# Turning q on VectorE too, in place, with half the blocks moved from a GpSimd copy

## The chip, the cores and the metric

The kernel runs on one core of one Trainium2 chip. A core has TensorE (matmuls, records PE, with weight loads PEld), VectorE (DVE), ScalarE (ACT), GpSimd (POOL) and SyncE (SP), which here only issues DMAs. All run their own instructions in order and wait for each other through semaphores. The metric is the device time of the whole kernel in microseconds (us); lower is better. Times of "before" are three runs; the profile is one more execution.

## The reference

Two parts, in float32. First attention over 8 batches and 8 heads, 576 tokens and 64 values per head, in which scores that lie more than `tau` below the row's maximum are dropped:

```python
scores = scale * np.matmul(q, k.transpose(0, 1, 3, 2))
thresh = np.max(scores, axis=-1, keepdims=True) - tau
scores = np.where(scores >= thresh, scores, -1000000000.0)
scores = scores - np.max(scores, axis=-1, keepdims=True)
attn = np.exp(scores)
attn = attn / (np.sum(attn, axis=-1, keepdims=True) + 1e-09)
return np.matmul(attn, v).astype(np.float32)
```

Its output, reordered to 4608 tokens of 512 values, goes through a feed-forward layer (512 to 1024 to 512) with a SoLU activation and a layer norm between:

```python
h = x @ w_in
e = np.exp(h - np.max(h, axis=-1, keepdims=True))
sm = e / (np.sum(e, axis=-1, keepdims=True) + 1e-09)
solu = h * sm
mu = np.mean(solu, axis=-1, keepdims=True)
var = np.mean((solu - mu) ** 2, axis=-1, keepdims=True)
ln = (solu - mu) / np.sqrt(var + 1e-06) * g_ln
return (ln @ w_out).astype(np.float32)
```

## The kernel before

**Tiling.** Two heads make a pair: head 0 on partitions 0 to 63, head 1 on 64 to 127. There are 32 pairs, numbered `i = 4 * batch + hp`. For scores, q and k must lie with the 64 values of a head along the partitions (`qT`, `kT`), while they come from memory with tokens along the partitions, so both must be turned. Of the 576 query tokens of a head, 512 are done in four slots of 128 (`kind` 0 and 1, `r` 0 and 1); the last 64, the tails (`qe`), of four pairs are gathered in two more slots (`kind` 2). This gives 18 slots per batch (`PER`) and 144 in all (`NS`).

**Rounds.** A hand-written loop at the end of the kernel issues everything for one slot per round, `rnd`; `tc.manual_schedule()` keeps the order. In round `rnd`:

- TensorE makes the scores of slot `rnd` (L451, two heads into two score banks `s_ps`). VectorE takes the maxima (`maxes`, L473), ScalarE the ramp that keeps or drops (L488), which is the last reader of a score bank, and the exponential (L497).
- GpSimd normalises the slot before (`normalise`, L504 to L507). VectorE turns it in 32x32 blocks (`blocks`, L519), and on every second slot four DMAs put it as `wT` (L530) where the product with v reads it, three rounds later (L555). ScalarE copies the product out to `xh` or `xe` (L578).
- TensorE also does a quarter of a feed-forward tile of 128 tokens: two rounds of first-layer halves (`ff_h`, L611), then two rounds of the output product (`ff_o`, L715). In between come, spread over later rounds, maximum and exponential (L626, L635), product (L641), statistics (`ff_stats`: L656 on VectorE, then five small GpSimd instructions), normalisation (`ff_norm` L677 on ScalarE, `ff_norm2` L682 on VectorE), a swap of blocks by four DMAs (`ff_swap`, L693, `V<-u`), and a VectorE transpose (`ff_turn`, L703, `uT`). Between two first-layer halves a small memset on GpSimd (`fence`, L108, `mark`) is waited for by TensorE.

**How q and k are turned.** For batches 0 and 1 TensorE multiplies 64x64 blocks by the identity (`turn`, L318), and ScalarE and VectorE copy the results from PSUM to `qT`, `kT`, `qe` (L351, L355, L376, L395, L399); q is scaled by `scl` on the way. In later rounds these products go to a spare part of the score banks, ahead of the scores of the same round; `preps` holds the items with their rounds.

From batch 2 on k goes another way. `load_natural` (L186) loads a pair of k in four DMAs of 32 partitions, three rounds ahead. `turn_natural` has VectorE transpose it in 32x32 blocks to a buffer `flip` (L191), and two DMAs bring it to `kT` (L194). Its place is the end of the round in `turn_at`: after `blocks` and the `late` jobs. q of these batches is still turned by TensorE: `load_one` loads half a batch (L130) and the tails (L141); `q_item` and `e_item` make 16 and 2 products per pair.

**Order of DMAs.** SyncE issues nearly all of them, in program order: in a round first the swap, then `wT`, the stores (L742), the flips, then loads by `load_at`. v comes in four parts per half batch (L158).

**Buffers.** `qT` has 6 buffers of 512 columns, `kT` 7, `qe` 7; `loads` has 2 for q and 2 for k.

Of the kernel before, what the change touches and what calls it, by code (L numbers as in the profile page):

```python
# [16 lines left out]
P = 128  # L17
# [3 lines left out]
def kernel(  # L21
# [127 lines left out]
    def load_v(b, hf, parts=(0, 1, 2)):  # L149
        d = halves.setdefault((b, hf), {})  # L150
        hs = slice(4 * hf, 4 * hf + 4)

        if b > 1:
            if 0 in parts:
                d["v"] = loads.tile([P, 4, NK, D], F32, tag="v", bufs=3, name="v")
            for part in parts:
                two, u = divmod(part, 2)
                nc.sync.dma_start(  # L158
                    out=d["v"][ROWS[u], 2 * two : 2 * two + 2].rearrange("p h m d -> p h (m d)"),
                    in_=v[b, hs][2 * two : 2 * two + 2].rearrange("h (p m) d -> p h (m d)", m=NK),  # L160
                )
            return
        if 0 in parts:
            d["v"] = loads.tile([P, 4, NK, D], F32, tag="v", bufs=3, name="v")
        rest = v[b, hs, 0:SM, :].rearrange("h (p t) d -> p h (t d)", t=4)
        for part, to, rows, of in (
            (0, 0, slice(0, P), slice(0, P)), (1, 4, ROWS[0], ROWS[1]), (1, 4, ROWS[1], ROWS[0])
        ):
            if part in parts:
                nc.sync.dma_start(  # L170
                    out=d["v"][rows, :, to : to + 4].rearrange("p h t d -> p h (t d)"),
                    in_=rest[of],
                )
        for rows in ROWS if 2 in parts else ():
            nc.sync.dma_start(
                out=d["v"][rows, :, NK - 1], in_=v[b, hs, SM:S, :].rearrange("h p d -> p h d")
            )

    def load_natural(i):
        b, hp = divmod(i, NP)  # L180
        src = k[b, 2 * hp : 2 * hp + 2].rearrange("h (i a t) d -> a h i (t d)", a=2, t=NK)
        raw = loads.tile([P, 4, 4, D], F32, tag="k", name="k")
        natural[i] = raw = raw.rearrange("p h t d -> p (h t d)")[:, 0 : NK * D]
        for g in range(4):
            a, h = divmod(g, 2)
            nc.sync.dma_start(out=raw[32 * g : 32 * g + 32], in_=src[a, h])  # L186

    def turn_natural(i):
        raw = natural.pop(i)
        flip = loads.tile([P, 2, NK, 32], F32, tag="flip", bufs=1, name="flip")  # L190
        nc.vector.transpose(out=flip, in_=raw.rearrange("p (t x g) -> p g t x", g=2, x=32))  # L191
        to = pair(i)["kT"]
        for a in range(2):
            nc.sync.dma_start(  # L194
                out=to[:, 32 * NK * a : 32 * NK * (a + 1)],
                in_=flip[ROWS[a]].rearrange("p g t x -> p g (t x)"),
            )

# [113 lines left out]
    def turn(spare, x, lhsT_of, rows=2):  # L312
# [3 lines left out]
        for r in range(rows):  # L316
# [14 lines left out]
    def pair(i):  # L331
        if i not in pairs:
            pairs[i] = dict(
                qT=heads.tile([P, SM], F32, tag="qT", bufs=6, name="qT"),
# [48 lines left out]
    def e_item(i):  # L383
        src, h0 = source(i)
        last = k_parts(i)[:, NK - 1] if i < 2 * NP else None

        def make(spare, x):
            turn(
                spare, x, lambda r, y: ends[i // NP][ROWS[r], 2 * (i % NP) + y],
                2 if i < 2 * NP else 1,  # L390
            )

        def keep(spare, x, r):
# [4 lines left out]
            elif last is not None:  # L398
# [31 lines left out]
    def scores(s, items):  # L430
# [10 lines left out]
        for ks in (slice(SM, S), slice(0, SM)):  # L441
            for h in range(2):
                for y in range(2):
                    if kind < 2:
                        d = pairs[b * NP + hp]
                        t = P * (2 * kind + r) + 64 * y
# [87 lines left out]
    def attend_steps(key):  # L534
# [7 lines left out]
        for e in range(2) if kind == 2 else [None]:  # L542
            for m in range(NK):
                for u in range(2):
                    d, h0 = source(b * NP + (hp if e is None else e + 2 * u))
                    for h in range(2):
                        if e is None:
                            to = y[ROWS[h], u, 0:P].rearrange("p (r g x) -> p g r x", r=2, g=2)
# [13 lines left out]
    def attended(key):  # L562
        b, kind, hp = key
        tag, y = units.pop(key)["y"]
        y = y.rearrange("p (u n) -> p u n", u=2)[:, :, 0:P].rearrange("p u (r y) -> p u r y", r=2)
# [6 lines left out]
        else:  # L572
# [4 lines left out]
            to = xh[b, kind][:, hp].rearrange("p (r u y) -> p u r y", r=2, u=2)  # L577
# [155 lines left out]
    def ff_store(t, last):  # L733
        d = ffn.pop(t)
        if len(t) == 1:
            rows = out.rearrange("(b s) m -> s b m", s=S)[SM:S, 2 * t[0] : 2 * t[0] + 2]
# [25 lines left out]
    for i in range(NP, NPAIR):  # L762
        b, hp = divmod(i, NP)
        if b == 1:
            at = (13, 15, 19, 20)[hp]
        else:
            at = PER * (b - 1) + ((6, 12, 16, 21) if b == 2 else (6, 9, 12, 17))[hp]
        if b == 1:
            preps += [
                (at, 3, lambda i=i: k_item(i, slice(0, 3)), i),  # L770
                (at, 1, lambda i=i: k_item(i, slice(3, 4)), i),
            ]
        preps += [
            (at, 1, lambda i=i: e_item(i), i),
# [4 lines left out]
    turn_at = {}  # L779
# [11 lines left out]
    for i in range(2 * NP, NPAIR):  # L791
        b, hp = divmod(i, NP)
        if b == 2:
            at = (24, 30, 34, 39)[hp]
        else:
            at = PER * b + 4 * hp - (11 if b % 2 else 13)
        turn_at[at] = i
        load_at.setdefault(at - 3, []).append(lambda i=i: load_natural(i))
        if hp % 2:
            load_at.setdefault(PER * (b - 1) + (9 if hp == 3 else -1), []).append(  # L800
                lambda b=b, hf=hp // 2: load_one(b, hf, "q")
            )
# [6 lines left out]
    with tc.manual_schedule():  # L809
# [29 lines left out]
        while True:  # L839
# [61 lines left out]
            if rnd - 1 in pieces:  # L901
                weight_c(pieces[rnd - 1])
            for job in middle.pop(rnd, []):
# [64 lines left out]
            if rnd in turn_at:  # L968
                turn_natural(turn_at[rnd])
            if rnd == 3:  # L970
# [47 lines left out]
```

## Time and profile before

| what | us |
|---|---|
| three runs | 885.73, 885.70, 883.92 |
| median | 885.7 |
| the profiled execution, whole | 883.54 |
| its span, first to last instruction | 881.8 |

The rows of the groups that the change touches, apart from those shown in the prediction:

```profile
L351 ACT ACTIVATE qT<-s_ps,scl 128x256 f32<-128x256 f32 x30 | 14.4, 481 | 0.0
L355 DVE TENSOR_SCALAR qT<-s_ps,scl 128x256 f32<-128x256 f32 x26 | 12.5, 480 | 0.0
L395 ACT ACTIVATE qe<-s_ps,scl 128x64 f32<-128x64 f32 x28 | 8.8, 313 | 0.0
L318 PE MATMUL s_ps<-ident,ends 64*64 64x64 f32 x128 | 8.5, 220 | 0.3 <-DVE both L473 0.3
```

A row names line, engine, operation, output and inputs, shapes and count; then the group's busy time in us and the mean of one in ns; then the idle time of the engine ahead of it and what ended it. Products in float32 appear twice, so 896 records of q are 28 pairs of 16 products. In a timeline a line gives start, length, engine, line and count; a bracket holds the idle time before it.

### The profile page before, as it was taken

The page shows a single profiled execution, that of the slowest core. Times are in us where ns is not written, and L with a number is a line of the kernel's source. Part 1 is how long each engine was busy: PE and PEld are TensorE (multiplying, and loading weights), DVE is VectorE, ACT ScalarE, POOL GpSimd, SP SyncE. Part 2 cuts the span into 40 slices and gives each one's busy share as a digit, 9 for nine tenths or more (in the row PEclk, how much of TensorE's full clock was granted, in tenths as well). Part 3 has the DMA queues.
Part 4 walks back from the last instruction along what each step waited for, and adds up shares of the span by engine and source line. Part 5 has one row for each costly group of instructions (what it writes and reads, how often), then busy time and mean ns, then how long its engine had stood idle before and what let it go on. Part 6 is the DMA issues. An engine that isn't in the chain of part 4 may idle for free. (4 is left out here: it accounts for less than half of the span.)

```text
span 881.8 us, 38016 instructions
## 1 busy us (share of the span) xinstructions
PE 835.4 (95%) x16225; PEld 592.1 (67%) x16225; DVE 682.0 (77%) x1248; ACT 586.3 (66%) x1201; POOL 471.0 (53%) x888
## 2 busy tenths in 40 slices
PE   5667999989999999999999999999999999999997
PEld 3445666665676877677777777777677677777655
DVE  5989788878787888888778887888687888777451
ACT  5977777767666766767677677777676777775121
POOL 2878655545555555555554655555555555555120
PEclk9878899999999999999999999999999999999999
DMA  7999978887878796988789787888779777866222
GB/s 230 254 260 256 218 186 196 217 191 175 201 170 212 178 208 157 206 207 189 158 194 214 184 204 166 208 213 185 165 173 219 182 174 155 186 133 143 65 49 49
DMA packets 85033, 161.60 MB, mean 183 GB/s; under 512 B 19832, under 2 KB 49536, under 8 KB 84864
## 3 DMA queue, kind: packets, MB, share of 16 engines
q1 hardware_dynamic: 83728, 157.18, 76.6%
q8 instruction: 127, 2.08, 1.1%
q10 hardware_dynamic: 1136, 2.00, 0.7%
q14 instruction: 42, 0.34, 0.1%
HBM read 46.14 MB, written 9.44 MB: 63 GB/s over the span
## 5 line engine op out<-in xcount | busy, mean ns | idle before, releaser
L473 DVE CUSTOM_DVE_ANT_0 w<-s_ps,tau_t 128x576 f32<-128x576 f32 x280 | 200.7, 754 | 108.0 <-PE s_ps L451 90.7
L715 PE MATMUL o_ps<-w,uT 64*64 64x256 f32 x4608 | 265.2, 376 | 1.1 <-DVE uT L703 1.1
L488 ACT ACTIVATE w<-s_ps,nth 128x576 f32<-128x576 f32 x280 | 199.8, 743 | 97.0 <-DVE nth L473 93.1
L715 PEld LDWEIGHTS o_ps<-w,uT 64*64 64x64 f32 x4608 | 218.9, 133 | 58.3 <-issue 13.8
L507 POOL TENSOR_SCALAR w<-w,sm 128x576 f32<-128x576 f32 x288 | 218.8, 772 | 14.3
L497 ACT ACTIVATE w<-w,ntau 128x576 f32<-128x576 f32 x288 | 220.3, 772 | 0.0
L611 PE MATMUL h_ps<-w,xh 64*64 64x512 f32 x1856 | 220.0, 596 | 0.0
L519 DVE STREAM_TRANSPOSE T<-w 128x576 f32<-128x576 f32 x288 | 206.3, 752 | 7.4 <-POOL w L507 6.0
L555 PEld LDWEIGHTS pv<-wT,v 64*64 64x64 f32 x5760 | 166.5, 136 | 51.1 <-issue 36.3
L451 PE MATMUL s_ps<-kT,qT 64*64 64x64 f32 (+1 forms) x2048 | 168.1, 422 | 16.4 <-ACT w L488 12.5
L555 PE MATMUL pv<-wT,v 64*64 64x128 f32 (+1 forms) x5760 | 170.9, 263 | 7.9 <-DMA wT<-T 3.7
L611 PEld LDWEIGHTS h_ps<-w,xh 64*64 64x64 f32 x1856 | 98.3, 135 | 96.6 <-issue 88.6
L504 POOL TENSOR_SCALAR sm<-sm 128x2 f32<-128x2 f32 x144 | 36.0, 250 | 229.5 <-ACT w L497 226.4
L505 POOL TENSOR_TENSOR sm<-sm,mone 128x2 f32<-128x2 f32 x144 | 104.6, 726 | 12.0
L677 ACT ACTIVATE V<-u,nb,rs 128x1024 f32<-128x1024 f32 x36 | 44.7, 1241 | 52.2 <-POOL nb L667 52.2
L451 PEld LDWEIGHTS s_ps<-kT,qT 64*64 64x64 f32 x2048 | 61.8, 139 | 25.1 <-ACT w L488 17.7
L578 ACT COPY xh<-pv 128x256 f32<-128x256 f32 x64 | 23.7, 370 | 67.3 <-PE pv L555 67.3
L703 DVE STREAM_TRANSPOSE uT<-V 128x1024 f32<-128x1024 f32 x36 | 44.5, 1236 | 23.7 <-DMA V<-u 23.5
L497 ACT ACTIVATION_READ_ACCUMULATOR w<-w,ntau 128x1 f32 x288 | 56.9, 198 | 0.0
L635 ACT ACTIVATE u<-h_ps,hm 128x1024 f32<-128x1024 f32 x36 | 40.2, 1118 | 21.2 <-DVE hm L626 15.3
L626 DVE TENSOR_REDUCE hm<-h_ps 128x1 f32<-128x1024 f32 x36 | 43.1, 1197 | 12.2 <-PE h_ps L611 6.2
L682 DVE TENSOR_SCALAR u<-u,rs,nb 128x1024 f32<-128x1024 f32 x36 | 42.4, 1178 | 12.7 <-ACT V L677 12.4
(82 smaller groups left out, 590.4 us busy)
## 6 DMA issues: line engine op xcount, KB each, us to landing
wT<-T SPq DMA_DIRECT2D x288, 288.0 KB, 5.9
v<-in_v_dram SPq DMA_DIRECT2D x48, 288.0 KB, 4.8
V<-u SPq DMA_DIRECT2D x144, 64.0 KB, 4.1
out_dram<-ob SPq DMA_DIRECT2D x71, 128.0 KB, 3.1
q<-in_q_dram SPq DMA_DIRECT2D x15, 512.0 KB, 5.9
k<-in_k_dram SPq DMA_DIRECT2D x96, 72.0 KB, 4.6
kT<-flip SPq DMA_DIRECT2D x48, 144.0 KB, 2.7
raw<-in_moe_w_out_dram SPq DMA_DIRECT2D x8, 512.0 KB, 8.2
```

The costliest lines, as they stand in the source:

```text
L451: nc.tensor.matmul(out=ps[h][ROWS[y], ks], lhsT=lhsT, rhs=d["kT"][ROWS[h], ks], start=True, stop=True,)
L473: nc.vector.tensor_tensor_reduce(out=w, in0=ps[:, 0:S], in1=(zero if loose else tau_t).to_broadcast([P, S]), scale=1.0, scalar=BIG, op0=AL ...
L488: nc.scalar.activation(out=d["w"][x], in_=d["w"][x] if d["loose"] else d["ps"][x][:, 0:S], func=AF.Prelu, bias=d["nth"][x], scale=-1.0, al ...
L497: nc.scalar.activation(out=w, in_=w, func=AF.Exp, bias=ntau, scale=1.0, accum_out=sm[:, x : x + 1])
L505: nc.gpsimd.tensor_tensor(out=sm, in0=sm, in1=mone, op=ALU.pow)
L507: nc.gpsimd.tensor_scalar(out=w, in0=w, scalar1=sm[:, x : x + 1], scalar2=1.0, op0=ALU.mult, op1=ALU.mult)
L519: nc.vector.transpose(out=T[:, :, r, h, :], in_=w)
L555: nc.tensor.matmul(out=to, lhsT=d["v"][ROWS[u], h0 + h, m ^ 4 * u if m < 8 and b < 2 else m], rhs=rhs, start=m == 0, stop=m == NK - 1,)
L611: mm = nc.tensor.matmul(out=h[ROWS[y], f], lhsT=x[ROWS[r], c, ROWS[y]], rhs=w1_parts[ROWS[r], c, part ^ r], start=part == 0 and c == 0, st ...
L677: nc.scalar.activation(out=V, in_=u, func=AF.Identity, bias=nb, scale=rs)
L703: nc.vector.transpose(out=uT, in_=d["V"].rearrange("p y (m x) -> p m y x", x=32))
L715: nc.tensor.matmul(out=d["o"][ROWS[z], 512 * r : 512 * r + 256], lhsT=d["uT"][ROWS[r], m].rearrange("p y x -> p (y x)"), rhs=w2[ROWS[r], m ...
```

## The change

From batch 2 on, q takes the way of k, and both take a shorter one:

- **Load.** One DMA for q and one for k per pair, 128 partitions of 9 tokens each (2304 bytes). q is loaded in the round of the previous turn, k a round later.
- **Scale.** GpSimd multiplies q by `scl` in the round of the turn, after `normalise`.
- **Turn.** VectorE transposes k and q in 32x32 blocks straight into `kT` and `qT`, one after the other at the end of the round. Half of the blocks then lie in the right place.
- **Copy and move.** A round later GpSimd copies both tiles to a twin (in a buffer of the `q` or `k` loads), and eight DMAs of 32 partitions by 288 columns bring the other half from the twin to its place.
- **Tails.** Five rounds after the turn GpSimd gathers the last block of each half of `qT` into `qe`.

The products, PSUM copies and half-batch loads of q for these batches go. `qT` grows to 576 columns, `flip` goes. The turn of pair 11 comes in round 36, not 39. Tokens now lie in another order in a pair, so v is loaded by another pattern (four DMAs of 32 partitions and four heads), the PV product and its copy keep another order, and the stores write rows accordingly, in pieces of 1 KB as before.

```diff
-    def load_natural(i):
+    def load_natural(i, nm):
         b, hp = divmod(i, NP)
...
-        for g in range(4):
-            a, h = divmod(g, 2)
-            nc.sync.dma_start(out=raw[32 * g : 32 * g + 32], in_=src[a, h])
+        raw = loads.tile([P, 4, 4, D], F32, tag=nm, name=nm)
+        natural[i, nm] = raw = raw.rearrange("p h t d -> p (h t d)")[:, 0 : NK * D]
+        src = {"q": q, "k": k}[nm][b, 2 * hp : 2 * hp + 2]
+        nc.sync.dma_start(out=raw, in_=src.rearrange("h (p t) d -> (h p) (t d)", t=NK))
+
+    def scale_natural(i):
+        raw = natural[i, "q"]
+        nc.gpsimd.tensor_scalar(
+            out=raw, in0=raw, scalar1=scl, scalar2=1.0, op0=ALU.mult, op1=ALU.mult
+        )
 
     def turn_natural(i):
-        raw = natural.pop(i)
-        flip = loads.tile([P, 2, NK, 32], F32, tag="flip", bufs=1, name="flip")
-        nc.vector.transpose(out=flip, in_=raw.rearrange("p (t x g) -> p g t x", g=2, x=32))
-        to = pair(i)["kT"]
-        for a in range(2):
-            nc.sync.dma_start(
-                out=to[:, 32 * NK * a : 32 * NK * (a + 1)],
-                in_=flip[ROWS[a]].rearrange("p g t x -> p g (t x)"),
+        for nm in ("k", "q"):
+            nc.vector.transpose(
+                out=pair(i)[nm + "T"].rearrange("p (g t x) -> p g t x", g=2, x=32),
+                in_=natural.pop((i, nm)).rearrange("p (t g x) -> p g t x", g=2, x=32),
             )
+
+    def copy_natural(i):
+        for nm in ("k", "q"):
+            twin = loads.tile([P, 4, 4, D], F32, tag=nm, name="twin")
+            natural[i, nm] = twin = twin.rearrange("p h t d -> p (h t d)")[:, 0 : NK * D]
+            nc.gpsimd.tensor_copy(out=twin, in_=pair(i)[nm + "T"])
+
+    def move_natural(i):
+        half = NK * 32
+        for nm in ("k", "q"):
+            to, twin = pair(i)[nm + "T"], natural.pop((i, nm))
+            for o in (0, 64):
+                for g in range(2):
+                    nc.sync.dma_start(
+                        out=to[o + 32 * g : o + 32 * g + 32, half * (1 - g) : half * (2 - g)],
+                        in_=twin[o + 32 * (1 - g) : o + 32 * (2 - g), half * g : half * g + half],
+                    )
+
+    def gather_ends(i):
+        d = pair(i)
+        last = d["qT"].rearrange("p (a t x) -> p a t x", a=2, x=32)[:, :, NK - 1]
+        nc.gpsimd.tensor_copy(out=d["qe"].rearrange("p (a x) -> p a x", a=2), in_=last)
...
-            at = (24, 30, 34, 39)[hp]
+            at = (24, 30, 34, 36)[hp]
         else:
             at = PER * b + 4 * hp - (11 if b % 2 else 13)
-        turn_at[at] = i
-        load_at.setdefault(at - 3, []).append(lambda i=i: load_natural(i))
+        load_at.setdefault(before, []).append(lambda i=i: load_natural(i, "q"))
+        load_at.setdefault(before + (at - before > 3), []).append(
+            lambda i=i: load_natural(i, "k")
+        )
+        turn_at[at] = ends_at[at + 5] = i
+        before = at
...
                 weight_c(pieces[rnd - 1])
+            if rnd in turn_at:
+                scale_natural(turn_at[rnd])
+            if rnd - 1 in turn_at:
+                copy_natural(turn_at[rnd - 1])
+            if rnd in ends_at:
+                gather_ends(ends_at[rnd])
...
             if rnd in turn_at:
                 turn_natural(turn_at[rnd])
+            if rnd - 1 in turn_at:
+                move_natural(turn_at[rnd - 1])
```

## The prediction

> **What bounds the kernel now.** I read the page's busy shares and slices first, then the stretch sums, then the groups with shapes kept apart, then the timeline by engine.
>
> ```profile
> PE 835.4 (95%) x16225; PEld 592.1 (67%) x16225; DVE 682.0 (77%) x1248; ACT 586.3 (66%) x1201; POOL 471.0 (53%) x888
> PE   5667999989999999999999999999999999999997
> PEclk9878899999999999999999999999999999999999
> ...
> core 0: us, PE busy (x) PEld busy (x) DVE busy (x) ACT busy (x) POOL busy (x), PEclk, DMA share, GB/s
> 200.00:800.00 600.00, 595.59 (x11984) 429.80 (x11980) 485.47 (x879) 419.75 (x854) 329.58 (x642) 1.00 0.81 186
> ```
>
> From 200 to 800 us TensorE is idle for 4.4 us, at full clock; VectorE has 115 us free there. But a busy TensorE is modelled, so I look at rounds, from one `s_ps` group to the next:
>
> ```profile
> 493.94 1.20 PE L451 MATMUL s_ps<-kT,qT 64*64 64x64 f32 x16
> 494.91 3.65 PE L611 MATMUL h_ps<-w,xh 64*64 64x512 f32 x32
> 498.35 2.19 PE L555 MATMUL pv<-wT,v 64*64 64x128 f32 x72
> 500.31 1.20 PE L451 MATMUL s_ps<-kT,qe 64*64 64x64 f32 x16
> ...
> 515.59 0.22 PE L318 MATMUL s_ps<-ident,ends 64*64 64x64 f32 x2
> ...
> 522.50 1.20 PE L451 MATMUL s_ps<-kT,qT 64*64 64x64 f32 x16
> ```
>
> A round of scores, a first-layer half and one PV product takes 6.37 us (500.31 less 493.94). The same round with a q item ahead of it takes 6.91 (522.50 less 515.59). These repeat: between 200 and 780 us the 24 rounds without an item have a median of 6.37 us, the 19 with one 6.90, and 50 rounds with an output step 4.43, with a spread of a tenth. Rounds that repeat to 0.1 us while the other engines' loads differ are set by TensorE. The work of one unit (two rounds of 6.37, two of 4.43) is 21.6 us.
>
> The other queues in the same stretch, SyncE's issues first:
>
> ```profile
> 488.28 3.71 SPq L186 DMA_DIRECT2D k<-in_k_dram  x4
> 492.04 0.64 SPq L158 DMA_DIRECT2D v<-in_v_dram  x1
> 495.00 4.25 SPq L530 DMA_DIRECT2D wT<-T  x4
> 499.35 3.00 SPq L693 DMA_DIRECT2D V<-u  x4
> 502.45 1.83 SPq L742 DMA_DIRECT2D out_dram<-ob  x2
> 504.40 1.22 SPq L194 DMA_DIRECT2D kT<-flip  x2
> ...
> 499.54 0.74 DVE L191 STREAM_TRANSPOSE flip<-k 128x576 f32<-128x576 f32 x1
> 501.55 0.76 DVE L473 CUSTOM_DVE_ANT_0 w<-s_ps,tau_t 128x576 f32<-128x576 f32 x1 [1.28 <-PE s_ps L451]
> 505.52 1.25 DVE L703 STREAM_TRANSPOSE uT<-V 128x1024 f32<-128x1024 f32 x1 [1.17 <-DMA V<-u]
> ```
>
> SyncE rests only from 492.68 to 495.00. VectorE ends the k turn 1.28 us before it is needed again. `uT` waits for its swap; it is ready at 506.77, and TensorE takes it at 507.66: 0.9 us of slack.
>
> **What the Trainium skill says.** "Perfetto Trace Analysis", Identifying the Most-Contended Engine, warns that matmul busy share is a poor measure of headroom; hence the rounds above, which agree with the busy share. The same page, What "DMA-bound" means, says an issuing sequencer that is solid with DMA slices is a bound of its own; SyncE is nearly that here. "VectorE: DVE Perf Modes", The three transpose paths: VectorE transposes 32x32 blocks only. The trace agrees in kind: `kT<-flip` moves must follow the 732 ns transpose. "GPSIMD Engine Reference", Performance versus the Vector engine, gives 1.03 cycles per element at best for short bodies and about 1.8 in an unrolled loop; used below.
>
> **The change part by part.** Rows for the prices:
>
> ```profile
> L318 PE MATMUL s_ps<-ident,q 64*64 64x64 f32 x896 | 21.6, 224 | 4.4 <-ACT qe L395 2.5 <-DVE both L473 1.3 <-ACT w L488 0.6
> L191 DVE STREAM_TRANSPOSE flip<-k 128x576 f32<-128x576 f32 x24 | 17.6, 732 | 0.0
> L507 POOL TENSOR_SCALAR w<-w,sm 128x576 f32<-128x576 f32 x288 | 218.8, 772 | 14.3
> ```
>
> *TensorE.* The 24 pairs of batches 2 to 7 lose 16 q products and 2 tail products each, 432 in all, each recorded twice. The row would give 768 records at 24.1 ns, 18.5 us, plus the tails. But a group's busy time runs under the pipelined start of the next one, so I take the round difference, which contains everything: 0.53 us x 24 = 12.8 us. The first four of these rounds (143 to 223 us) lie where TensorE is not full (66.7 of 70 us from 130 to 200), but they stand in its queue too; one of them waits 0.5 us more. Nothing is added to TensorE; the 64x128 PV output becomes contiguous, with as many columns: taken as 0, between -1 and +1 us.
>
> *ScalarE* loses per pair a 128x256 copy (481 ns) and a 128x64 one (313 ns), 19 us in all, both between its two ramps. It is not the bound: worth nothing directly, but the second ramp, which frees the score bank, comes 0.8 us sooner.
>
> *VectorE* loses a 480 ns scaled copy per pair and gains a second transpose of 732 ns: +0.25 us, 6 us in all. Nearly every turn keeps its place at the end of a round with `u` (L682). There the spare 1.28 us becomes about 0.55 after one more transpose, where no item stood in that round; where one stood, its 480 ns go while the round shrinks by 0.53, and 1.28 would again come to about 0.5. It fits. One turn moves, that of pair 11, from round 39 to 36: there it comes after `ff_mul`, in a 4.43 us round that VectorE already fills, so 1.5 us late there; I charge 1 us once.
>
> *GpSimd* gains per pair a q scaling like L507 (772 ns), two 128x576 copies, and a 128x64 gather. The trace has no copy. Bounds: 576 elements at the page's 1.03 and 1.8 cycles at 1.2 GHz give estimates of 0.49 and 0.86 us; L507 has the same shape, so 0.77. The gather is estimated at 0.25 from the 250 ns of L504. Sum 2.6 us per pair, 62 us, raising POOL to about 533 us. The scaling stands behind the normalisation and ahead of `mark`, the fence that the second first-layer half needs; at 498.75 the fence ran, and its user started at 501.29, so 0.77 us is covered. The copies (1.5 us) stand ahead of the next normalisation, which follows 2.5 us of idleness in such rounds (505.43). Covered. A wait for the q load would hold all of these, but it is issued a turn, some 20 us, ahead.
>
> *SyncE and the DMAs.* Per pair it loses four k loads (3.0 to 3.7 us), two flips (1.22), half a q load and a quarter of the tail loads (0.5). It gains two whole loads, 0.6 each like the q load, and eight moves of 32 rows x 1152 B. The nearest row is `V<-u`, also 32 rows from SBUF: 590 ns median and 0.75 us each with what holds it up. So 8 x 0.64 (with the gap) = 5.1, up to 6.2. Net +1.5 us per pair, between +0.9 and +2.7. Moved bytes stay equal (k once and q once from HBM, 288 KB moved inside), and most packets get longer, so the engines' 0.81 share stays. The moves wait for copies which end near 504.5 in this stretch, whereas SyncE reaches them after `wT`, about 509: no wait. Behind them stand the next k load, then `wT` of the next unit, then `V<-u`. The rest before 495.00 is 2.3 us; less 0.53 for the shorter unit and 1.5, some 0.3 us remain. At the upper price `wT` and `V<-u` come 0.9 us late, just the slack of `uT`. The v loads (two heads by 64 rows become four by 32, same bytes) and the stores (1 KB pieces as before) cost nothing new.
>
> *The start and the tail* are untouched: up to 130 us both kernels issue nearly the same, and the last chain (norm, swap, `o_ps` of 7.17 us) is the same.
>
> *Sum.* The profiled execution took 883.5 us (span 881.8). 883.5 - 12.8 + 1 (the displaced turn) + 0.5 (SyncE now and then late) = 872.2. The three times have a median of 885.7, 2.2 above the profiled one; two of three lie there, so I add 1.3: 873.5.
>
> **The rivals.**
> *VectorE or SyncE eats part of it* (877 to 883.9). For: slacks of 0.3 to 0.9 us at four places per unit. Against: 115 us free on VectorE. If each pair loses 0.3 us, 7 us go: about 880.
> *SyncE becomes the bound: slower.* Place: the queue before `wT` and `V<-u`. Once lag exceeds 0.9 us, `uT` and so the output step come late; the pair loses the excess. It turns slower when the excess passes 0.53, that is at a net cost of 1.8 + 0.9 + 0.5 = 3.2 us per pair, 0.5 above my upper bound. With moves at 0.9 us each (1.5 + 2.1 = 3.6 net) each pair loses 0.9 against 0.53: 24 x 0.4 = 9 us, 895. For: `wT` issues were seen to take 1 us each in this stretch. Against: hold-ups follow bytes, which don't grow.
> *More than the sum* (under 870): ScalarE's relief also ends the 12.5 us that `s_ps` waits for the ramp L488, most of it early. At half, 6 us: 867.5.
> That the products do not vanish can be excluded: no code path makes them for batches 2 to 7.
>
> **How the numbers follow.** Forecast (870 to 877) 0.48, more 0.08, part eaten 0.20, no change 0.06, slower 0.18. Within 0.2% (883.9 to 887.5) is about what a measurement can tell from no change. Faster 0.48 + 0.08 + 0.20 = 0.76. The range from 868 to 886 holds the forecast, the eaten part, most of "more" and most of "no change": 0.80; the slower case stays out.
>
> **What would show it.** Right: rounds with a first-layer half at 6.37 us throughout from 200 us, no L318-like group after 130 us, PE busy some 13 us less, `uT` waits for `V<-u` no longer than 23.5 us in sum by much, GpSimd near 533 us. Wrong: TensorE waiting for `uT` or `wT`, VectorE waiting for k or q, SyncE without any rest, or GpSimd copies far above 0.9 us.

## The result and the profile after

The changed kernel took 927.0 us (median of 6 runs, 924.2 to 932.0); the kernel before, on the same chip, 885.7 us (6 runs, 881.5 to 888.2). The ratio is 1.0475, with a 95% interval of 1.0433 to 1.0517: slower by some 42 us. The profiled execution took 930.5 us, its span 928.7. The forecast was 873.5 us, with a range of 868 to 886: the time moved the other way and lies outside the range.

First the page of after: busy times with shares of the span, then two rows of the 40 slices.

```profile
PE 841.8 (91%) x15361; PEld 623.7 (67%) x15361; DVE 689.0 (74%) x1248; ACT 572.5 (62%) x1153; POOL 528.1 (57%) x984
...
PE   5667999898789999899989999899998999999997
PEclk9779999999899999899998999899999999999999
```

TensorE has 864 instructions fewer, and yet it is "busy" 6 us longer. Its slices are no longer a row of nines: an 8 or a 7 stands every few slices, and most of the 8s in the granted clock stand under or beside one.

The groups of the parts that the change added, with shapes kept apart:

```profile
L188 POOL TENSOR_SCALAR q<-q,scl 128x576 f32<-128x576 f32 x24 | 17.8, 742 | 3.8 <-DMA q<-in_q_dram 3.8
L194 DVE STREAM_TRANSPOSE qT<-q 128x576 f32<-128x576 f32 x24 | 17.7, 736 | 0.0
L203 POOL COPY twin<-qT 128x576 f32<-128x576 f32 x24 | 15.9, 664 | 0.0
L219 POOL COPY qe<-qT 128x64 f32<-128x64 f32 x24 | 5.7, 236 | 0.0
```

All four were priced within 0.01 us or too high (0.77, 0.73, 0.77 and 0.25 us), and 528 us on GpSimd against 533 forecast says the same. So the loss isn't in the work of the engines. The waits say where it is; a row has engine, line, what is waited for, then the sum in us, how often, and the longest. First two of before, then four of after:

```profile
DVE uT L703 <- DMA V<-u: 23.5, 21, 4.1
PE pv L555 <- DMA wT<-T: 3.7, 6, 1.3
...
DVE uT L728 <- DMA V<-u: 50.6, 23, 5.0
PE pv L577 <- DMA wT<-T: 18.0, 15, 4.7
PE pv L577 <- DMA v<-in_v_dram: 15.0, 6, 3.9
DVE kT L194 <- DMA k<-in_k_dram: 5.7, 4, 2.5
```

The last two have no counterpart in before. All four are waits for a DMA, and all of those are issued by SyncE. TensorE itself stands at v and at `wT`; for `uT` it waits 3.0 us in all, so most of VectorE's longer wait for the swap doesn't reach it directly.

Round by round (from one group of scores to the next, as in the prediction) the gain is there. Rounds with a first-layer half take 6.37 us where nothing stalls, and there each that had held a q item is 0.53 to 0.58 us shorter. But a few rounds are far longer. Five of them, one per batch from 2 to 6, take 12.3 to 13.0 us instead of 6.37, 32 us more in sum; one takes 14.2 instead of 8.2; and a dozen lose 1 to 3 us. Batch by batch from batch 2 on, the lag behind before at the start of the batch is 1.2, 17.0, 21.9, 30.4, 36.4 and 44.2 us.

One of the five long rounds, the tenth of batch 3, in the timeline of after:

```profile
371.12 3.66 SPq L211 DMA_DIRECT2D kT<-twin  x4
...
374.87 3.55 SPq L211 DMA_DIRECT2D qT<-twin  x4
...
378.47 0.66 SPq L158 DMA_DIRECT2D v<-in_v_dram  x1
...
379.17 0.59 SPq L184 DMA_DIRECT2D k<-in_k_dram  x1
...
379.81 0.65 SPq L158 DMA_DIRECT2D v<-in_v_dram  x1
...
382.84 0.44 PE L577 MATMUL pv<-wT,v 64*64 64x128 f32 x4 [1.88 <-DMA v<-in_v_dram]
...
383.95 0.78 DVE L194 STREAM_TRANSPOSE kT<-k 128x576 f32<-128x576 f32 x1 [2.06 <-DMA k<-in_k_dram]
...
385.42 3.89 PE L577 MATMUL pv<-wT,v 64*64 64x128 f32 x66 [2.14 <-DMA v<-in_v_dram]
```

Read it from the top. The eight moves hold SyncE for 7.3 us. Only then come two v loads and a k load. In program order the later v load belongs to the eighth round of the batch; it is issued in the tenth. TensorE takes up the product with v, waits 1.88 us for one part of v, makes 4 records, and waits 2.14 us for the other. VectorE meanwhile waits for k. The 66 products then take 3.89 us, where the group of 72 in the prediction took 2.19. The sums of three stretches show why (start and end, length, busy us and count of PE, PEld, DVE, ACT, POOL; then the granted clock, the DMA share, GB/s):

```profile
340.00:370.00 30.00, 29.29 (x620) 22.79 (x616) 24.55 (x44) 19.75 (x40) 19.26 (x37) 1.00 0.78 184
375.00:390.00 15.00, 10.97 (x164) 8.19 (x160) 7.68 (x14) 6.70 (x14) 9.44 (x19) 0.80 0.74 165
390.00:410.00 20.00, 20.00 (x340) 14.03 (x336) 16.48 (x31) 13.50 (x26) 10.23 (x20) 0.98 0.73 175
```

TensorE's granted clock is 0.80 in the stretch of the waits and 1.00 ahead of it. Here waits of 4.0 us in sum go with a round of 12.6 us instead of 6.37.

The round of 14.2 us, in batch 2, has another wait:

```profile
225.56 4.00 SPq L211 DMA_DIRECT2D kT<-twin  x4
229.67 2.43 SPq L211 DMA_DIRECT2D qT<-twin  x4
...
232.82 3.16 SPq L718 DMA_DIRECT2D V<-u  x4
236.09 3.57 SPq L551 DMA_DIRECT2D wT<-T  x4
...
243.68 0.46 PE L577 MATMUL pv<-wT,v 64*64 64x128 f32 x4 [4.72 <-DMA wT<-T]
```

The issues of `wT` stand behind eight moves and a swap, and the product waits 4.72 us for them to land. These are the moves of pair 11. They start 12.2 us after those of pair 10, since the change brought this pair's turn from round 39 to 36; all other pairs are 21 us or more apart.

### The profile page after: what moved, and what is told of

It is laid out like the page before. It is cut to its first block, busy times and chain, and to the rows that moved or that the text cites. A ratio compares the mean times of both kernels' runs of the same rounds, so it can differ in the third digit from the quotient of the medians.

```text
span 928.7 us, 36438 instructions
## 1 busy us (share of the span) xinstructions
PE 841.8 (91%) x15361; PEld 623.7 (67%) x15361; DVE 689.0 (74%) x1248; ACT 572.5 (62%) x1153; POOL 528.1 (57%) x984
## 5 line engine op out<-in xcount | busy, mean ns | idle before, releaser
L740 PE MATMUL o_ps<-w,uT 64*64 64x256 f32 x4608 | 271.8, 376 | 5.7 <-DVE uT L728 3.0
L740 PEld LDWEIGHTS o_ps<-w,uT 64*64 64x64 f32 x4608 | 214.6, 133 | 70.1 <-issue 13.7
L509 ACT ACTIVATE w<-s_ps,nth 128x576 f32<-128x576 f32 x280 | 196.8, 741 | 99.2 <-DVE nth L494 93.3
L577 PEld LDWEIGHTS pv<-wT,v 64*64 64x64 f32 x5760 | 186.6, 143 | 85.8 <-issue 46.3
L528 POOL TENSOR_SCALAR w<-w,sm 128x576 f32<-128x576 f32 x288 | 226.1, 796 | 14.3
L577 PE MATMUL pv<-wT,v 64*64 64x128 f32 (+1 forms) x5760 | 193.0, 275 | 44.1 <-DMA wT<-T 18.0
L636 PE MATMUL h_ps<-w,xh 64*64 64x512 f32 x1856 | 223.3, 590 | 0.3 <-ACT ob L755 0.3
L472 PE MATMUL s_ps<-kT,qT 64*64 64x64 f32 (+1 forms) x2048 | 181.9, 429 | 16.7 <-ACT w L509 14.0
L636 PEld LDWEIGHTS h_ps<-w,xh 64*64 64x64 f32 x1856 | 120.9, 134 | 73.7 <-issue 38.6
L472 PEld LDWEIGHTS s_ps<-kT,qT 64*64 64x64 f32 x2048 | 75.8, 142 | 25.3 <-ACT w L509 19.6
L728 DVE STREAM_TRANSPOSE uT<-V 128x1024 f32<-128x1024 f32 x36 | 44.5, 1237 | 50.9 <-DMA V<-u 50.6
L671 POOL TENSOR_SCALAR se<-se 128x1 f32<-128x1 f32 x36 | 8.4, 233 | 97.7 <-ACT u L660 97.4
```

Source lines behind the costliest of these rows:

```text
L472: nc.tensor.matmul(out=ps[h][ROWS[y], ks], lhsT=lhsT, rhs=d["kT"][ROWS[h], ks], start=True, stop=True,)
L509: nc.scalar.activation(out=d["w"][x], in_=d["w"][x] if d["loose"] else d["ps"][x][:, 0:S], func=AF.Prelu, bias=d["nth"][x], scale=-1.0, al ...
L528: nc.gpsimd.tensor_scalar(out=w, in0=w, scalar1=sm[:, x : x + 1], scalar2=1.0, op0=ALU.mult, op1=ALU.mult)
L577: nc.tensor.matmul(out=to, lhsT=d["v"][ROWS[u], h0 + h, m ^ 4 * u if m < 8 and b < 2 else m], rhs=rhs, start=m == 0, stop=m == NK - 1,)
L636: mm = nc.tensor.matmul(out=h[ROWS[y], f], lhsT=x[ROWS[r], c, ROWS[y]], rhs=w1_parts[ROWS[r], c, part ^ r], start=part == 0 and c == 0, st ...
L728: nc.vector.transpose(out=uT, in_=d["V"].rearrange("p y (m x) -> p m y x", x=32))
```

## The experiments

Two suspects came out of the trace. **V**, the v cut: before, a part of v held two heads on one half of the partitions, so that the third pair of a batch needed only the two parts issued in rounds 4 and 5. In after a part holds all four heads on a quarter of the rows, so every pair needs all four parts, and the last is still issued in round 7. **S**, SyncE's time for eight moves per pair. The rival, **R**: VectorE's second transposes or GpSimd's copies come late for another engine.

### The v cut

`v_early` issues after's four v loads of the second half batch in one round:

```diff
-            at, by = (PER * b + 4, 1) if hp == 3 else (PER * b - 9, 2)
+            at, by = (PER * b + 4, 0) if hp == 3 else (PER * b - 9, 2)
```

> Theory V: the changed kernel loses its time where the first pair of the second half batch waits for v, because each of the four v parts now holds a quarter of the rows of all four heads, so the last part, issued one round ahead, is needed at once. Theory S: it loses it because SyncE's queue is too full with the eight moves, so that everything it issues comes late. This kernel is the changed one, with the four parts of the second half batch issued together in round 4 of their batch instead of in rounds 4, 5, 6 and 7. V: five of the stalls of some 6 us go, 30 us or more, to 890 to 897 us or lower. S: no transfer less is issued, so 920 us or more.

Measured: 920.3 us, ratio 1.042 (1.036 to 1.048), the number expected of S. Yet TensorE no longer waits for v. Instead four loads together on SyncE push back the swap `V<-u`: VectorE waits 62.8 us for it in sum, and three output rounds of the odd batches take 9.1 to 10.0 us instead of 4.43. The stall moved rather than went, so this run doesn't price V.

`before_vcut` is the kernel before with only the v cut changed (a part takes 32 adjacent partitions; in after it is every second one of 64):

```diff
-                two, u = divmod(part, 2)
+                c, u = divmod(part, 2)
...
-                    out=d["v"][ROWS[u], 2 * two : 2 * two + 2].rearrange("p h m d -> p h (m d)"),
-                    in_=v[b, hs][2 * two : 2 * two + 2].rearrange("h (p m) d -> p h (m d)", m=NK),
+                    out=d["v"][64 * u + 32 * c : 64 * u + 32 * c + 32].rearrange("p h m d -> p h (m d)"),
+                    in_=v[b, hs].rearrange("h (c p m) d -> c p h (m d)", c=2, m=NK)[c],
```

> The kernel before, with the v loads alone cut as in the changed kernel: each part a quarter of the rows of all four heads, in place of two heads' rows on one half of the partitions; same bytes, same rounds. V: the PV product of the third pair of a batch waits for the part issued one round ahead, some 4 to 6 us in each of six batches, so 905 to 920 us. S: 886 us, within 2 us of before, since there are no moves here and as many DMAs.

Measured: 902.0 us, ratio 1.021 (1.016 to 1.026), a little under V's range, with nothing of q or k touched. Its waits:

```profile
PE pv L555 <- DMA v<-in_v_dram: 13.5, 4, 4.7
PEld pv L555 <- DMA v<-in_v_dram: 4.9, 1, 4.9
```

The ninth rounds of batches 2, 4 and 6 take 13.3, 13.0 and 12.2 us; the odd batches, whose product comes a round later, have no stall. V is shown, and alone it costs before some 18 us.

`v_due` gives the loads the due times that their new cut asks for, and doesn't bunch them:

```diff
-            at, by = (PER * b + 4, 1) if hp == 3 else (PER * b - 9, 2)
+            at, by = (PER * b + 2, 1) if hp == 3 else (PER * b - 9, 2)
```

> The kernel after, but the four v loads of the second half batch go two rounds sooner (rounds 2, 3, 4 and 5 of a batch instead of 4 to 7), so that the last is issued in the round in which the kernel before issued the last one that its third pair needed, and no two in one round. Theory (v cut with unmoved due times, plus SyncE's time): the stalls of TensorE for v go, as in v_early, but without v_early's bunching; SyncE's extra time for the moves remains. Expected 900 to 912 us, the waits of TensorE for v under 3 us in sum, rounds of 6.37 us in the even batches' ninth place. Rival (SyncE's time is all, v is a symptom): no better than v_early, about 920 or more.

Measured: 908.8 us, ratio 1.0275 (1.0234 to 1.0316). The waits for v are gone from the list, and the five long rounds with them (that of batch 2 with the wait for `wT` stays, at 14.8 us). So V is 2.0% of after's 4.75%; the other 2.75%, and the 1.4% that TensorE gained, are something else. Its waits:

```profile
DVE uT L728 <- DMA V<-u: 63.2, 28, 5.4
PE pv L577 <- DMA wT<-T: 22.3, 25, 5.4
```

### SyncE's time

`no_moves` leaves out GpSimd's copies and the eight moves, so that half of the blocks of `qT` and `kT` are not in place:

```diff
-            if rnd - 1 in turn_at:
-                copy_natural(turn_at[rnd - 1])
...
-            if rnd - 1 in turn_at:
-                move_natural(turn_at[rnd - 1])
```

> The changed kernel without the copies to the twin and without the eight moves per pair (half of the blocks of qT and kT stay in the wrong place; left out is just this work). V: the v loads keep their rounds; they come a little sooner as the queue is emptier, but most of the stall stays: 900 to 915 us. S: all of the loss goes, 873 to 878 us.

Measured: 899.2 us, ratio 1.018 (1.0124 to 1.0236), 2.8% under after's. The three stalls for v in even batches remain (13.2, 11.8 and 11.1 us), those in odd batches go, and `uT` waits 30.5 us for the swap (before 23.5, after 50.6). So the odd-batch stalls of after need both: V, and loads pushed late by S. The run takes the copies away together with the moves, but the trace of after parts them: for every one of the 24 pairs the copy had ended 1.6 to 11.9 us before SyncE issued the first move, so SyncE never waited for a copy there.

`v_early_no_moves` is v_early without copies and moves (the same work is left out):

> The changed kernel with the v parts of the second half batch all in round 4, and without the copies to the twin and the eight moves (half of the blocks of qT and kT stay in the wrong place; left out is just this work). Theory VS: the loss of the changed kernel is these two causes and nothing else, the cut of v and the time that the moves take in SyncE's queue; with both gone the 12.8 us of TensorE work that was taken away must show: 872 to 877 us. Rival R: something else in the change costs (the second transpose on VectorE, the GpSimd scaling and gather, the other order of tokens): 880 us or more.

Measured: 893.7 us, ratio 1.010 (1.0063 to 1.0136), which is the number expected of R. But three output rounds take 9.9 to 10.0 us instead of 4.43, 17 us more in sum, and in each the four bunched v loads stand on SyncE just ahead of `V<-u`. They are v_early's own cost; without the 17 us the time would be an estimated 877 us.

`before_flip8` adds nothing but issues to the kernel before: its two flips per pair become eight, with the same bytes.

```diff
-            nc.sync.dma_start(
-                out=to[:, 32 * NK * a : 32 * NK * (a + 1)],
-                in_=flip[ROWS[a]].rearrange("p g t x -> p g (t x)"),
-            )
+            for j in range(4):
+                nc.sync.dma_start(
+                    out=to[32 * j : 32 * j + 32, 32 * NK * a : 32 * NK * (a + 1)],
+                    in_=flip[64 * a + 16 * j : 64 * a + 16 * j + 16].rearrange("p g t x -> p g (t x)"),
+                )
```

> The kernel before with each of the two k flips cut into four DMAs, so 8 issues of 36 KB in place of 2 of 144 KB per pair, with the same bytes and rows. Theory VS: the six more issues, about 4 us per pair of SyncE's time, use up its rest and make wT and V<-u late, as the moves do in the changed kernel: 895 to 920 us. Rival R (SyncE has room, the loss lies elsewhere): 886 us, within 3 us of before.

Measured: 950.3 us, ratio 1.073 (1.068 to 1.078), far above what was expected. Two of its waits:

```profile
DVE uT L704 <- DMA V<-u: 56.8, 26, 5.5
PE pv L556 <- DMA wT<-T: 30.8, 28, 5.0
```

These are the two waits that grew in after, without q on VectorE, without GpSimd's copies and with v as before. More issues on SyncE are enough; R isn't needed for them. (TensorE also waits 8.7 us for late q loads here; in after it doesn't turn q from batch 2 on.)

### Other queues for the same DMAs

Could another engine issue them? `v_early_moves_act` has ScalarE issue the moves of v_early (`nc.scalar.dma_start` in `move_natural`):

> The changed kernel with the v parts of the second half batch all in round 4, and the eight moves issued by ScalarE in place of SyncE. V: as v_early, within 3 us, unless the ScalarE issues (eight times about 0.6 us per pair) delay its ramps. S: SyncE is rid of the moves, so this one is faster than v_early by 10 us or more.

Measured: 1092.2 us, ratio 1.236 (1.229 to 1.243). ScalarE issues in order too: a pair's eight moves hold it for 8.9 us on average, although their copies were done 2 us or more before the first. Its ramps (L509) wait 159 us in sum behind moves of q, and TensorE waits for the score banks that the ramps free.

Two kernels put the output stores on ScalarE, `before_st` with the kernel before, `after_st_v` with after and with v's second half batch issued in rounds 4, 4, 5 and 6 of the even batches:

```diff
-            (nc.scalar if last and z else nc.sync).dma_start(
+            nc.scalar.dma_start(
```

> The kernel before, with all output stores issued by ScalarE. VS: TensorE is full already, so 882 to 888 us, no change within 0.5%. If ScalarE's issues delay its ramps, 890 us or more.

> The changed kernel with the output stores issued by ScalarE, and the v parts of the second half batch issued in rounds 4, 4, 5 and 6 in even batches (4, 5, 6, 7 in odd ones, where the PV product that needs them comes a round later). VS: SyncE gets back 1.85 of the 3.1 us per pair that the moves cost, and the last v part lands before its use: 880 to 900 us. If SyncE's time is not the cause of the late transfers, the stores change nothing: 905 us or more.

Measured: before_st 909.1 us, ratio 1.029 (1.025 to 1.033), since the ramps are late again: rounds of 4.43 us become 5.91. after_st_v took 902.9 us, ratio 1.023 (1.019 to 1.028), just above the range expected. The same stores on ScalarE cost before 26 us, yet with v a little earlier they go with 2.4% less than after. That fits V and S, but two edits are in it.

`v_due_pool` and `v_due_pool_qk` use GpSimd: the first for v (with its second half batch in rounds 3 to 6), the second for q and k too.

```diff
-                nc.sync.dma_start(
+                nc.gpsimd.dma_start(
                     out=d["v"][64 * u + c : 64 * u + 64 : 2].rearrange("p h m d -> p h (m d)"),
```

> The kernel after with the v loads of batches 2 to 7 issued by GpSimd instead of SyncE, the second half batch's a round sooner than in after. SyncE is rid of two v loads per pair, 1.3 us, which takes the net addition from 3.1 to about 1.8 us per pair, below the break-even of 3.2 and close to the predicted 1.5. Theory (SyncE's time is what is left of the loss): 880 to 895 us. Rival (issuing costs the engine that does it as much as it cost ScalarE in before_st): GpSimd's normalisations come late and TensorE waits for w or for the fence, 905 or more.

> As v_due_pool, with the q and k loads of batches 2 to 7 issued by GpSimd too. SyncE is rid of about 1.3 us per pair more, so its net addition is some 0.5 us per pair. Theory (SyncE's time): the gain of TensorE's rounds shows at last, 870 to 882 us. Rival (GpSimd can't take the issues): slower than v_due_pool.

Both missed. Measured: 902.2 us, ratio 1.020 (1.017 to 1.024), and 917.4 us, ratio 1.035 (1.030 to 1.041). The group row of the v loads in v_due_pool_qk:

```profile
L158 POOL DMA_DIRECT2D v<-in_v_dram x48 | 30.4, 634 | 2.6 <-PE pv L577 2.3 <-issue 0.3
```

GpSimd is held 0.63 us for each, and is busy 556 and 585 us where v_due has 528. It is the engine that normalises `w` and makes the statistics of the feed-forward part; in v_due_pool_qk `uT` waits 70.0 us for the swap and TensorE 20.7 us for `uT`. So neither run shows what SyncE's relief is worth alone: each mixes it with a new load on GpSimd.

### Fewer moves

The first try at fewer DMAs, `flip_q`, turns q the way before turned k: transpose into a second buffer, then two flips of 144 KB for each of q and k, no copies and no moves, and v cut by heads as before.

> A third version: q turned by VectorE from batch 2 on, as in the changed kernel, with one load each for q and k, the GpSimd scaling and the gather, but each turned tile brought to its place by two DMAs of 144 KB, as k was before, without twin and moves; v is cut by pairs as before. Per pair SyncE issues 6 DMAs (before: 6.75, changed: 10), 288 KB more are moved. Theory VS: neither cause is there, so the 12.8 us show: 870 to 877 us, faster than both. Rival R: 880 us or more, as the second transpose and the GpSimd work are still there.

Measured: 1095.7 us, ratio 1.238 (1.235 to 1.241). VectorE waits 128.6 us for loads of k, up to 16.4 us for one. The fault was in the load: one DMA whose source begins with a dimension of 2. "DMA: Bandwidth & Descriptors" of the Trainium skill, Why a DMA increments its semaphore by 16 and not by 1, says that the largest number up to 16 which divides the slowest dimension of both sides is the number of DMA engines used; that would be 2 here, an estimate. The next run has each load as two DMAs of 64 partitions:

```diff
-        nc.sync.dma_start(out=raw, in_=src)
+        for a in range(2):
+            nc.sync.dma_start(out=raw[ROWS[a]], in_=src[a])
```

> As flip_q, but q and k of a pair loaded by two DMAs of 64 partitions each instead of one whose source begins with a dimension of 2. In flip_q VectorE waited 128.6 us for the k loads and both kernels' cuts of v and moves were absent, so the expectation of flip_q was about another thing. Theory VS with room on SyncE (8 issues per pair, about 4.8 us, against 4.65 before): 872 to 882 us. Rival R (the second transpose and the GpSimd work cost TensorE time): 890 us or more with waits of TensorE for VectorE or GpSimd in the trace.

Measured for `flip_q2`: 888.3 us (9 runs), ratio 1.0066 (1.0039 to 1.0093), between the two ranges expected. The slow loads are cured but for 8.5 us of waits for k, at most 4.2 us each, which agrees with the page. The count of packets under 512 B agrees too: flip_q2 has 17240 and flip_q 15800, and 1440 more is what 96 loads with 16 each make in place of 48 with 2. Neither V nor moves are left, and the q item rounds are 0.57 us shorter. But `uT` still waits longer for the swap (36.6 us from 200 to 800 us, before 17.0 there), TensorE stands still for 13.0 us in that stretch (before 4.4), and the gain doesn't show. How much each wait takes of it wasn't traced. `flip_q2_st`, with the stores on ScalarE, made it worse, as before_st had:

> As flip_q2, with all output stores issued by ScalarE, which makes the tile they store, so SyncE has 1.85 us less per unit of four rounds. VS: another 0 to 8 us faster than flip_q2, 868 to 878 us. R: no faster, or slower by the ScalarE issues.

Measured: 933.8 us, ratio 1.058 (1.054 to 1.062).

The second try keeps the change's own way. In `joint` and `joint_right` q and k of a pair lie side by side in one tile of 2 x 576 columns, as do their copies; one DMA then moves a block row of both, and eight moves become four of twice the size. v is loaded as in v_due. `qT` has a seventh buffer by this, and to make room `ends` and two small tiles have fewer. In joint the transposes read their blocks in another order, so that its scores are made of other blocks; the instructions and DMAs are as many.

```diff
-            qT = heads.tile([P, S], F32, tag="qT", bufs=6, name="qT")
+            both = heads.tile([P, 2, S], F32, tag="qk", name="qk")
...
-        for nm in ("k", "q"):
-            to, twin = pair(i)[nm + "T"], natural.pop((i, nm))
-            for o in (0, 64):
-                for g in range(2):
+        to, twin = pair(i)["both"], natural.pop((i, "twin"))
+        for o in (0, 64):
+            for g in range(2):
...
-                        out=to[o + 32 * g : o + 32 * g + 32, half * (1 - g) : half * (2 - g)],
-                        in_=twin[o + 32 * (1 - g) : o + 32 * (2 - g), half * g : half * g + half],
+                    out=to[o + 32 * g : o + 32 * g + 32, :, half * (1 - g) : half * (2 - g)],
+                    in_=twin[o + 32 * (1 - g) : o + 32 * (2 - g), :, half * g : half * g + half],
```

> v_due, and q and k of a pair lie side by side in one tile, so that one DMA moves a block row of both: four moves of 32 partitions by two times 1152 bytes per pair, not eight of 1152, with the same bytes. The tile of qT and kT has seven buffers, so qT has one more than in after; the two sorts of loads keep the products, transposes and copies as they are. SyncE is rid of four issues per pair, about 3.2 us, so its net addition per pair goes from 3.1 us to about 0. Theory (v's due times and the issue time of the moves are the cause): the predicted gain appears, 868 to 884 us, TensorE waits for wT below 8 us, uT waits for V<-u near the 23.5 us of before. Rival (the wait is on what is moved, the bytes or the 32-partition packets, not on the count of issues): no better than v_due_pool, about 900 us. Second rival (GpSimd's or VectorE's additions are late): rounds grow at waits for w, T or the fence.

> joint with the transpose reading its input blocks in the order of after (joint read them in the order they lie in, so that its scores were made of other blocks; every instruction and DMA count is the same). Theory (v's due times and the issue time of the moves): 876 to 884 us, as joint, a few us below before; TensorE's waits for v and wT stay under 6 us in sum. Rival (the order in which the transpose reads costs VectorE time): the transposes take longer than 0.74 us each and the time rises above before.

Measured: joint 880.6 us (20 runs), ratio 0.9953 (0.9933 to 0.9973). joint_right, with the block order of after, 881.9 us (22 runs), ratio 0.9964 (0.9943 to 0.9985). It is faster than both kernels, before by 0.15% to 0.57%, after by some 5%. Its busy row and its waits:

```profile
PE 825.5 (94%) x15361; PEld 615.8 (70%) x15361; DVE 689.1 (78%) x1248; ACT 573.0 (65%) x1153; POOL 529.8 (60%) x984
```

```profile
DVE uT L732 <- DMA V<-u: 37.8, 26, 5.3
PE pv L581 <- DMA wT<-T: 5.0, 9, 1.7
```

VectorE and GpSimd do what they do in after, in as much time, and the loss is gone: R falls as its cause. The seventh buffer isn't what helps: in v_due the transposes into `qT` wait for nothing (0.0 us). The moves make as many packets of 1152 bytes as in v_due, 6144, in half the DMAs, so it isn't the packets either. TensorE is busy 16 us less than in after for the same instructions. `joint_late_v` puts v's loads back to after's rounds:

> joint_right with the v loads of the second half batch back at after's rounds 4 to 7. The issue time on SyncE is then cured and the v cut is not: what v's due times cost by themselves. Theory (the two causes add): 16 to 18 us more than joint_right, as in before_vcut, so 893 to 902 us, with the ninth round of even batches at 12 to 13 us and odd batches without a stall. Rival (v stalls only because SyncE is late): within 5 us of joint_right.

Measured: 904.6 us, ratio 1.019 (1.012 to 1.025), 2.2% above joint_right and a little over what was expected. The ninth rounds of batches 2, 4 and 6 take 13.4, 12.5 and 11.2 us; one odd batch has a partial stall of 2.7 us, which was not expected. V costs as much with four moves as in before_vcut, where there are none.

### What a microsecond of SyncE costs

The trace gives the length of each record of SyncE. The table sums those of the DMAs over the same work in each kernel, from the twelfth to the sixty-seventh group of `wT` issues; the moves or flips of all 24 pairs lie in it.

| kernel | stretch, us | issuing, us | more than before, us | the same per pair, us |
|---|---|---|---|---|
| before | 609.3 | 487.1 | 0 | 0 |
| before_vcut | 626.9 | 481.4 | -5.6 | -0.2 |
| before_flip8 | 669.3 | 585.9 | 98.9 | 4.1 |
| after | 651.7 | 558.6 | 71.6 | 3.0 |
| v_due | 631.8 | 554.0 | 67.0 | 2.8 |
| flip_q2 | 610.0 | 517.4 | 30.3 | 1.3 |
| joint_right | 604.9 | 498.7 | 11.6 | 0.5 |

From v_due to joint_right issuing falls by 55.4 us and the stretch by 26.9: 0.5 us for each us. From before to before_flip8 issuing grows by 98.9 us and the stretch by 60.0: 0.6 for each. The rate is rough: it comes from two pairs of traces, and a record also holds the time in which its issue is held up, which is partly an effect of a full queue. With 0.5 to 0.6, after's additional 71.6 us are an estimated 36 to 43 us. With V at 18 and TensorE's gain of 13, that makes 41 to 48 us; the stretch grew by 42. flip_q2, with 30.3 us and no V, comes to +2 to +5 by the same sum; its stretch grew by 1.

## Why the prediction was wrong

*TensorE, -12.8 us*: right by the round (24 times 0.53 is 12.7). Former item rounds fell by 0.53 to 0.58 us, and the other rounds kept 6.37 and 4.43 us, wherever nothing stalled. *ScalarE, VectorE, GpSimd*: right in size and in being covered; the copy, which the trace of before did not have, took 0.66 us, inside the bounds of 0.49 and 0.86. joint_right has the same work on all three and none of the loss.

*The v loads "(two heads by 64 rows become four by 32, same bytes) ... cost nothing new"*: this step failed. It priced bytes and issues, which indeed stayed equal, and didn't ask when each part is first needed. After the cut the third pair needs the part issued two rounds later than the last that it needed before, and that part wasn't moved. before_vcut, v_due and joint_late_v agree on its price: 2.1%, 2.0% and 2.2%, some 18 to 20 us. No rival held this mechanism.

*SyncE, net +1.5 us per pair, at most +2.7*: mis-sized, and the larger part of the loss. The moves were priced at 0.64 us; between 200 and 780 us they took 0.87 (k) and 0.73 (q) on average, 0.80 together, so eight take 6.4 us, above the upper price of 6.2. Over the whole queue it came to 3.0 us per pair.

*The break-even, 3.2 us net per pair*: the second error in the same step. It was worked out from one stretch in which SyncE rested 2.3 us and `uT` had 0.9 us to spare. The rival "SyncE becomes the bound" had the right place, the queue ahead of `wT` and `V<-u`, and by its own price the measured 3.0 us would have left the time near before. v_due, with 2.8 us per pair and V cured, is 24 us slower than before all the same. There was no common rest to use up first: in before SyncE issues for 487 of the 609 us of the table's stretch, in order, and part of its remaining time is itself waiting for work that is late (`wT` for the transposed `T`, 113.6 us in the whole of before and 83.9 in after). A stretch with room in one round pays nothing to a round that has two stores and a v load. On v and on SyncE together the forecast took two independent small risks; the trace shows them adding, and in the odd batches needing each other.

*The displaced turn, +1 us on VectorE*: wrong in kind. With the turn in round 36 the moves of pairs 10 and 11 crowd on SyncE, and rounds 39 and 40 take 24.2 us in after and 24.4 in v_due, 15.2 in before and 15.5 in no_moves. These 9 us are a good third of what v_due loses; no run puts the turn back to round 39.

The Trainium skill, "DMA: Bandwidth & Descriptors", Issuing engines are not separate DMA queues, says that the time a sequencer takes to initiate a DMA is usually small relative to the DMA itself. Here a move takes 0.80 us to issue, and from issue to landing 4.1 us (k) or 2.7 (q) in the median: a fifth to a third of it. But the issues stand in one queue, and it is their sum that delays what stands behind. The measurement decides.

*"Hold-ups follow bytes, which don't grow"*, the argument against that rival: refuted by before_flip8 (same bytes, +65 us) and by joint_right (same bytes in half the DMAs, -27 us against v_due).

What stays open: joint_right gains 3 us of the 13. `uT` waits 37.8 us for the swap there, before 23.5, and SyncE still issues 11.6 us more in all. At 0.5 to 0.6 us for each that explains an estimated 6 to 7 us; the rest wasn't traced to a cause. How much of each long round is the wait and how much the lower clock behind it wasn't parted by a run. Merging k's and q's moves with the v cut of before wasn't tried.

## What to carry to other kernels

When a load is cut another way, ask for each part when it is first needed, not only how many bytes it has: the same bytes in the same rounds cost 2% here. Count DMAs on an in-order issuing queue like instructions on an engine, at the mean time of their records, hold-ups included, and don't take slack seen in one stretch for slack in all. If the bytes must be moved anyway, lay tiles side by side so that one DMA carries two: that, with a few buffers resized, turned a loss of 2.8% into a gain of 0.4%.

## What was not expected of the hardware

The length of an issue hardly followed size here. Three issue rows of after (count, KB each, median us from issue to landing):

```profile
v<-in_v_dram SPq DMA_DIRECT2D x48, 288.0 KB, 4.5
...
k<-in_k_dram SPq DMA_DIRECT2D x24, 288.0 KB, 3.3
...
kT<-twin SPq DMA_DIRECT2D x96, 36.0 KB, 4.1
```

Between 200 and 780 us SyncE was held 0.80, 0.62 and 0.87 us on average by one of them, and 0.90 us by the moves of 72 KB in joint_right. Further:

- A v load issued by GpSimd held GpSimd for 0.63 us (v_due_pool_qk); 71 stores moved to ScalarE cost 26 us (before_st), and a row of eight moves held ScalarE for 8.9 us (v_early_moves_act).
- In a stretch of 15 us with waits of 1.88 and 2.14 us TensorE's granted clock was 0.80, and 66 products took 3.89 us (after).
- Loads whose source begins with a dimension of 2 kept VectorE waiting up to 16.4 us (flip_q); as two DMAs of 64 partitions at most 4.2 us (flip_q2).
